# Bringing two column slices of the first input tile by a transposing DMA instead of by TensorE transposes

## The chip, the cores and the metric

The kernel runs on one core of one Trainium2 chip. The metric is the device time of one execution in microseconds (us). A profile is one execution recorded by the hardware profiler; its span is some 2 us shorter than the timed figure.

Names used below: PE is TensorE (matmul), PEld its weight load, DVE is VectorE, ACT is ScalarE, SPq is the queue of SyncE, which issues all DMAs of this kernel. An ft is one of the twelve tiles of 128 columns of w1; four of them make a block. The trace records sixteen landings for each DMA, and these are called its parts.

## The reference, cut to what matters

```python
# x [1, 2048, 640], w1 [640, 1536], w2 [1536, 640], all bf16
h   = silu(einsum("bsd,df->bsf", x, w1))
out = einsum("bsf,fd->bsd", h, w2)
# outputs: out and the gradients of x, w1 and w2 for a given grad_out
```

The kernel works through the 2,048 rows in four chunks of 512. The change concerns only how the first chunk of x gets ready.

## The kernel before

The matmul contracts over the 640 columns of x, which must therefore lie on the partitions: x has to be transposed. Later chunks come by a transposing DMA. For the first chunk, x is loaded as it lies (`x_two`, in two halves of 256 rows), and TensorE transposes it in 128 x 128 pieces. Meanwhile TensorE is kept busy with 22 warm-up matmuls that nobody reads.

```python
KM = 2
NWARM = 22
...
for i in range(NWARM):
    early.append(nc.tensor.matmul(wp[:, 0:P], lhsT=warm[:], rhs=warm[:], start=True, stop=True))
...
early += [load_x_half(0), load_x_half(1), load_w1_rows(0, 1), load_w1_rows(1, KM)]
load_w1_rows(KM, DT)                       # first w1 block: columns 0..511, 5 row slices
start_before_entry_wait(nc, {i.ins.name for i in early})
for fc in range(1, NFC):
    load_w1(fc * FC, (fc + 1) * FC)        # second and third w1 block, 655 KB each
...
nc.sync.dma_start(out=w2_nat[:], in_=w2_v[:])
goT_next = load_goT(0)                     # a transposing DMA
...
def pe_x_half(xT, half):
    lo = half * 2 * P
    for dt_ in range(DT):                  # DT = 5 column slices
        tp = ps_h.tile([P, 2, P], dt_in, name="tp", tag="hp")
        for q in range(2):
            nc.tensor.transpose(tp[:, q, :], x_two[:, half, q, dt_ * P:(dt_ + 1) * P], ident[:])
        copy = nc.scalar.copy if dt_ % 2 else nc.vector.tensor_copy
        copy(out=xT[:, dt_, lo:lo + 2 * P].rearrange("p (s q) -> p q s", q=2), in_=tp[:])

pe_x_half(xT_next, 0)
pe_x_half(xT_next, 1)
...
def h_first(xT, aT, ghT):
    # ft = 0..3 (first w1 block): slices 0..KM-1 for all four, then KM..4 for each;
    # ft = 4..7 need the second w1 block, ft = 8..11 the third
```

So the first 20 hidden-layer matmuls (four ft, five slices) live on the first w1 block. The 21st, the first of ft=4, needs the second block.

## Time and profile before

| | before |
|---|---|
| time, median (first three runs) | 321.44 us |
| span of the profile | 319.4 us |
| PE busy | 314.6 us, 98% |
| both halves of x landed | 3.14 and 4.02 us |
| first hidden-layer matmul | 5.30 us |
| second w1 block: eight of its sixteen parts landed, last part landed | 7.33 us, 9.91 us |
| weight load of the 21st hidden-layer matmul (ft=4) | 9.95 us |

The first excerpt is from the page of before: the span, the busy time of the engines, the chain that ended last by engine and by line, and the group of hidden-layer matmuls (count, busy us, mean ns of one, idle time before them).

```profile
span 319.4 us, 3541 instructions
...
PE 314.6 (98%) x1469; PEld 146.3 (46%) x1498; DVE 102.6 (32%) x182; ACT 77.9 (24%) x142; POOL 0.7 (0%) x6
...
PE 98%; DMA 1%; issue 1%; DVE 0%; DVEq 0%; SPq 0%
PE hp L269 32%; PE hp L206 16%; PE hp L357 16%; PE hp L253 16%; PE hp L406 15%; PE hp L387 1%; DMA x_two<-in_x_dram 1%; PE tp L197 1%; DVE g L398 0%; DVEq L398 0%; SPq L434 0%
...
L206 PE MATMUL hp<-xT,w_nat 128*128 128x512 bf16 x238 | 57.2, 381 | 0.1
```

The chain is PE nearly everywhere. The 1,440 matmuls' worth of work runs 216 ns apart once settled, which is 311 us, so only about 8 us of the span can be won at all, and most of that is the start. The mean of 381 ns is the length of one pipelined matmul, not its spacing.

The chain in order of time, its first pieces (start us, us, what):

```profile
0.09 3.06 DMA x_two<-in_x_dram
3.19 2.31 PE tp L197 x20
5.50 1.93 PE hp L206 x7
7.49 10.74 PE hp L206 x49
```

It starts with the load of x, goes to the 20 transposes, then to matmuls. Now the timeline of the first 12 us (start us, duration us, engine, line, operation, in brackets the idle time before and what ended it):

```profile
0.09 0.87 SPq L173 DMA_DIRECT2D x_two<-in_x_dram  x2
...
1.00 1.44 SPq L178 DMA_DIRECT2D w_nat<-in_w_dram  x3
...
2.48 1.06 SPq L169 DMA_DIRECT2D w_nat<-in_w_dram  x2
...
3.19 2.31 PE L197 MATMUL tp<-ident,x_two 128*128 128x128 bf16 x20 [0.16 <-DMA x_two<-in_x_dram]
...
5.03 12.15 SPq L162 DMA_TRANSPOSE goT<-in_grad_out_dram  x1
...
5.30 6.88 PE L206 MATMUL hp<-xT,w_nat 128*128 128x512 bf16 x28
...
9.95 1.95 PEld L206 LDWEIGHTS <-w_nat 128*128 128x128 bf16 x10 [0.21 <-DMA w_nat<-in_w_dram]
```

Two things are to be seen. TensorE goes from transposes to matmuls without a hole. And the last line shows that the weight load at 9.95 us, the one for ft=4, waited 0.21 us for a DMA of w1: work and data are about level there. PE itself lost nothing by it: its matmuls stay 216 ns apart across that point.

Third, the stretches of one microsecond (us, then busy time of PE, PEld, DVE, ACT and POOL with counts, granted clock, share of the DMA engines, GB/s moved). The view books a packet's whole time and bytes where the packet starts, so a share can pass 1:

```profile
4.00:5.00 1.00, 1.00 (x13) 1.00 (x11) 1.00 (x4) 0.81 (x3) 0.00 (x0) 1.00 0.98 324
5.00:6.00 1.00, 1.00 (x7) 0.60 (x6) 0.99 (x3) 0.77 (x2) 0.00 (x0) 1.00 0.99 347
6.00:7.00 1.00, 1.00 (x5) 0.44 (x4) 0.00 (x0) 0.00 (x0) 0.00 (x0) 1.00 0.97 324
```

The DMA engines are full: 324 to 347 GB/s at a share of 0.97 to 0.99.

### The profile page before, as it was taken

Reading aid. Unit: us, or ns where it says so; the run is one execution under the profiler, and the core shown is the slowest. Engines: PE = TensorE matmul, PEld = TensorE weight load, DVE = VectorE, ACT = ScalarE, POOL = GpSimd, SP = SyncE. Lnnn points to the kernel's source line nnn. Section 1 sums busy time; section 2 is a strip of 40 time slices with the busy share of each in tenths; the row PEclk is TensorE's granted clock in tenths of the full one; section 3 lists DMA queues with packets and bytes.
Section 4 is the critical chain, followed back from the end, with each engine's and each line's share of the span. In section 5 each row is a group of like instructions: output and inputs, shape, how many; then the busy total and the mean of one; then the engine's idle time right before and its main releaser. Section 6 shows DMA issues by size and latency. Waiting matters only on the chain.

```text
span 319.4 us, 3541 instructions
## 1 busy us (share of the span) xinstructions
PE 314.6 (98%) x1469; PEld 146.3 (46%) x1498; DVE 102.6 (32%) x182; ACT 77.9 (24%) x142; POOL 0.7 (0%) x6
## 2 busy tenths in 40 slices
PE   9999999999999999999999999999999999999996
PEld 6444444444444444444444444444444444444443
DVE  3771541477410087710147741000000100001001
ACT  4960000545201254411054520110100001001100
POOL 0000000000000000000000000000000000000000
PEclk9999999999999999999999999999999999999999
DMA  8999999999999855292634079819999998995111
GB/s 282 307 180 222 246 292 264 341 263 292 293 278 271 223 190 140 86 308 76 171 114 133 2 259 267 217 30 294 265 212 257 267 240 292 253 294 182 49 37 45
DMA packets 147312, 67.33 MB, mean 211 GB/s; under 512 B 112609, under 2 KB 147041, under 8 KB 147297
## 3 DMA queue, kind: packets, MB, share of 16 engines
q1 hardware_dynamic: 147296, 67.12, 80.9%
q8 instruction: 11, 0.18, 0.2%
q14 instruction: 5, 0.03, 0.0%
HBM read 9.83 MB, written 28.97 MB: 121 GB/s over the span
## 4 chain that ended last, share of the span: by engine, by line
PE 98%; DMA 1%; issue 1%; DVE 0%; DVEq 0%; SPq 0%
PE hp L269 32%; PE hp L206 16%; PE hp L357 16%; PE hp L253 16%; PE hp L406 15%; PE hp L387 1%; DMA x_two<-in_x_dram 1%; PE tp L197 1%; DVE g L398 0%; DVEq L398 0%; SPq L434 0%
## 5 line engine op out<-in xcount | busy, mean ns | idle before, releaser
L206 PE MATMUL hp<-xT,w_nat 128*128 128x512 bf16 x238 | 57.2, 381 | 0.1
L253 PE MATMUL hp<-goT,w2T 128*128 128x512 bf16 x232 | 56.4, 379 | 0.4
L269 PE MATMUL hp<-aT,w_nat 128*128 128x512 bf16 x235 | 52.2, 379 | 0.3
L269 PE MATMUL hp<-ghT,w1T 128*128 128x512 bf16 x235 | 52.2, 379 | 0.3
L357 PE MATMUL hp<-a_blk,go_nat 128*128 128x512 bf16 x236 | 51.8, 379 | 0.2
L406 PE MATMUL hp<-gh_blk,x_nat 128*128 128x512 bf16 x219 | 48.2, 379 | 0.3
L277 ACT ACTIVATE oT<-hp 128x512 bf16<-128x512 f32 x24 | 14.3, 598 | 109.8 <-PE hp L269 109.8
L215 ACT ACTIVATE aT<-hp 128x512 bf16<-128x512 f32 x48 | 29.9, 625 | 33.0 <-PE hp L206 33.0
L206 PEld LDWEIGHTS <-w_nat 128*128 128x128 bf16 x240 | 23.6, 99 | 28.4 <-issue 0.6
L269 PEld LDWEIGHTS <-w1T 128*128 128x128 bf16 x240 | 23.5, 98 | 28.3
L357 PEld LDWEIGHTS <-go_nat 128*128 128x128 bf16 x240 | 23.5, 98 | 28.3
L253 PEld LDWEIGHTS <-w2T 128*128 128x128 bf16 x240 | 23.5, 98 | 28.3
L269 PEld LDWEIGHTS <-w_nat 128*128 128x128 bf16 x240 | 23.5, 98 | 28.4
L279 DVE CAST oT<-hp 128x512 bf16<-128x512 f32 x16 | 11.1, 692 | 77.0 <-PE hp L269 63.5
L260 DVE SCALAR_TENSOR_TENSOR ghT<-ghT,hp 128x512 bf16<-128x512 bf16 x48 | 32.5, 682 | 7.3 <-PE hp L253 7.3
L406 PEld LDWEIGHTS <-x_nat 128*128 128x128 bf16 x224 | 21.9, 98 | 26.4
L222 DVE SCALAR_TENSOR_TENSOR ghT<-aT,v 128x512 bf16<-128x512 bf16 x48 | 32.8, 687 | 0.5
L221 DVE TENSOR_SCALAR v<-t 128x512 bf16<-128x512 f32 x48 | 20.3, 426 | 30.5 <-ACT t L219 30.5
L219 ACT ACTIVATE t<-hp 128x512 f32<-128x512 f32 x48 | 29.8, 625 | 0.0
L417 DVE CAST g<-hp 128x512 bf16<-128x512 f32 x7 | 4.8, 692 | 47.0 <-PE hp L406 27.4
L367 DVE CAST g2T<-hp 128x512 bf16<-128x512 f32 x7 | 4.8, 692 | 46.1 <-PE hp L357 46.1
L365 ACT ACTIVATE g2T<-hp 128x512 bf16<-128x512 f32 x8 | 4.8, 597 | 47.0 <-PE hp L357 40.8
(20 smaller groups left out, 27.0 us busy)
## 6 DMA issues: line engine op xcount, KB each, us to landing
aT_scr<-aT SPq DMA_DIRECT2D x4, 1536.0 KB, 6.2
ghT_scr<-ghT SPq DMA_DIRECT2D x4, 1536.0 KB, 8.0
out_dram<-o_sb SPq DMA_DIRECT2D x8, 640.0 KB, 3.6
oT_scr<-oT SPq DMA_DIRECT2D x4, 640.0 KB, 3.6
go_nat<-in_grad_out_dram SPq DMA_DIRECT2D x4, 640.0 KB, 6.4
x_nat<-in_x_dram SPq DMA_DIRECT2D x4, 640.0 KB, 5.3
gxT_scr<-oT SPq DMA_DIRECT2D x4, 640.0 KB, 4.7
w_nat<-in_w_dram SPq DMA_DIRECT2D x1, 1920.0 KB, 13.4
```

What stands on the lines that cost most here:

```text
L206: nc.tensor.matmul(hp[:], lhsT=w1_nat[:, dt_, ft * P:(ft + 1) * P], rhs=xT[:, dt_, :], start=(dt_ == 0), stop=(dt_ == DT - 1),)
L215: nc.scalar.activation(aT[:, ft, :], hp[:], ACT.Silu)
L219: nc.scalar.activation(t[:], hp[:], ACT.Tanh, scale=0.5)
L221: nc.vector.tensor_scalar(out=v[:], in0=t[:], scalar1=-0.5, scalar2=0.5, op0=ALU.mult, op1=ALU.add)
L222: nc.vector.scalar_tensor_tensor(out=ghT[:, ft, :], in0=aT[:, ft, :], scalar=1.0, in1=v[:], op0=ALU.subtract, op1=ALU.mult)
L253: nc.tensor.matmul(gp[:], lhsT=w2T[:, dt_, ft * P:(ft + 1) * P], rhs=goT[:, dt_, :], start=(dt_ == 0), stop=(dt_ == DT - 1),)
L260: nc.vector.scalar_tensor_tensor(out=ghT[:, ft, :], in0=ghT[:, ft, :], scalar=1.0, in1=gp[:], op0=ALU.add, op1=ALU.mult)
L269: nc.tensor.matmul(op_[:], lhsT=w_all[:, ft, dt_ * P:(dt_ + 1) * P], rhs=rhs_all[:, ft, :], start=(ft == 0), stop=(ft == FT - 1),)
L277: nc.scalar.activation(oT[:, dt_, :], op_[:], ACT.Copy)
L279: nc.vector.tensor_copy(out=oT[:, dt_, :], in_=op_[:])
L357: nc.tensor.matmul(gp[:], lhsT=go_nat[:, st, dt_ * P:(dt_ + 1) * P], rhs=a_blk[:, st, :], start=(st == 0), stop=(st == ST - 1),)
L406: nc.tensor.matmul(gp[:], lhsT=x_nat[:, st, dt_ * P:(dt_ + 1) * P], rhs=gh_blk[:, st, :], start=(st == 0), stop=(st == ST - 1),)
```

## The change

The intent: take 8 of the 20 transposes and 4 of the 10 copies away from the start. Column slices 3 and 4 of x come by one transposing DMA, placed in the queue behind the first three w1 slices. `KM` becomes 3, so that slices 3 and 4 are needed later. The remaining copies write without a stride.

```diff
-    KM = 2
-    NWARM = 22
+    KM = 3
+    NWARM = 24
+    KT = 3
...
-        early += [load_x_half(0), load_x_half(1), load_w1_rows(0, 1), load_w1_rows(1, KM)]
-        load_w1_rows(KM, DT)
+        early += [load_x_half(0), load_x_half(1), load_w1_rows(0, 1), load_w1_rows(1, KT)]
+        nc.sync.dma_start_transpose(out=xT_next[:, KT:DT, :], in_=x2[0:SC, KT * P:D])
+        load_w1_rows(KT, DT)
...
-            for dt_ in range(DT):
+            for dt_ in range(KT):
...
-                copy(out=xT[:, dt_, lo:lo + 2 * P].rearrange("p (s q) -> p q s", q=2), in_=tp[:])
+                copy(out=xT[:, dt_, lo:lo + 2 * P], in_=tp[:].rearrange("p q s -> p s q"))
```

`x_two` still loads all five column slices, so 512 x 256 elements of x (262 KB) now cross the DMA engines twice.

## The prediction

> **What bounds the kernel now.** TensorE. The page gives PE busy 314.6 of 319.4 us (98%), and the chain of waits is PE for 98%. The chain shows 49 matmuls in 10.74 us, about 216 ns each; 1,440 of them are 311 us. Only some 8 us of the span are other than full-rate matmuls, 5.3 us of them the start, all that the change touches.
>
> **The start of before (timeline and landings).** x half 0 has landed at 3.14 us, half 1 at 4.02. The 20 transposes run from 3.19, 107 ns apart, and the first hidden-layer matmul begins at 5.30. The first three are 420-430 ns apart, from 6.41 on they are 216 ns apart: the array is cold until then. The Trainium skill ("TensorE: Matmul & The Clock Gate", Part 1) puts a cold array at half rate, with a free-running window before it speeds up; the trace agrees (107 ns for 128 columns, 427 for 512). The 21st matmul (ft=4) starts at 10.08. It needs the second w1 block, whose last sixteenth lands at 9.91 (its weight load waited 0.21 us for that DMA); the other fifteen landed by 8.23. So there matmul work and DMA are level already. DMA is saturated: 0.88 to 1.07 busy, 320 to 376 GB/s from 1.5 to 14 us.
>
> **Removes.** 8 transposes (8 x 107 = 0.86 us) and 4 PSUM copies (0.45 us each, DVE and ACT in parallel). Not all is gained: half 1 lands only at 4.02. I expect the first matmul near 5.0, 0.3 us earlier. With dt 0..2 first, the 12 matmuls last to about 8.2, part of them cold.
>
> **Adds.** x still loads whole, so 262 KB more go through a full queue, ahead of the rest of w1. In this trace transposing DMAs run at 290 GB/s at best, so at least 0.9 us. A w2T transpose (655 KB) took 3.1-3.7 us of SyncE issue; scaled, some 1.4 us, so the two last w1 slices are issued near 3.4 instead of 2.0. I estimate xT landing at 6-7.3 us and those slices at 6.5-8.5: level with the need near 8.2. The second w1 block moves from 9.91 to 10.5-11.8. The two more warm-up matmuls are filler.
>
> **On the critical path.** The earlier matmuls then run into the later second w1 block: ft=4 starts near 11.0 instead of 10.08, and everything behind shifts by that. The third block (11.8 us before, needed near 14.4) and w2 (17.0, needed at 18.7) keep their slack. Sum: about +0.9 us.
>
> **Predicted: 322.3 us, range 321.0 to 323.6.** Faster by over 2%: 0.01; within 2%: 0.97; slower by over 2%: 0.02.
>
> **What would show each step.**
> - First hidden-layer matmul at 4.8-5.1 us.
> - xT's transposing DMA landing at 6-7.3 us; second w1 block about 0.6-1.9 us later than 9.91.
> - In the waits, PE or its weight load waits 0.5-1.8 us for w1 before ft=4.
> - From 20 us on, matmul spacing and busy times unchanged; the shift constant to the end.
>
> **What would make it wrong.** (1) The one late DMA engine: if the lag is not there in unprofiled runs, the second block is early enough, and the change gains 0.2-0.4 us. (2) The transposing DMA may hold up the other engines' packets: when goT's begins, packets nearly stop from 15.4 to 16.5 us (24 GB/s in one slice of the DMA view) and w2's sixteen parts land together at 17.0. The same in mid-stream would cost 1-2 us more, and a wait before dt 3. (3) A PE gap could bring the half-rate clock back, 0.2 us per matmul. (4) The cold period may end at another moment (free-running window): 0.2-1 us either way.

## The result, and the profile after

| | before | after |
|---|---|---|
| time, median of 4 runs each (lowest to highest) | 321.28 (321.12 to 321.49) us | 322.34 (321.84 to 322.93) us |
| ratio after : before | | 1.0033, 95% interval 1.0014 to 1.0052 |

A difference given in us below as "above before" is ratio minus one times the median of before of the same rounds. The change costs about 1.1 us, 0.3%. That is "same" at the 2% line, but clear of noise: the interval does not reach 1.

The page after, the same lines (the changed file has two lines more, so L206 of before is L208 here):

```profile
span 321.1 us, 3533 instructions
...
PE 316.1 (98%) x1463; PEld 146.0 (45%) x1492; DVE 101.4 (32%) x180; ACT 76.9 (24%) x140; POOL 0.7 (0%) x6
...
PE 97%; DMA 1%; issue 1%; DVE 0%; SPq 0%; DVEq 0%
PE hp L271 32%; PE hp L208 17%; PE hp L255 16%; PE hp L359 16%; PE hp L408 15%; DMA x_two<-in_x_dram 1%; PE hp L389 1%; DVE xT L201 0%; PE tp L199 0%; SPq L174 0%; DVE g L400 0%; DVEq L400 0%; SPq L436 0%
...
L208 PE MATMUL hp<-xT,w_nat 128*128 128x512 bf16 x233 | 58.7, 390 | 0.5
```

The hidden-layer matmuls have a mean of 390 instead of 381 ns: some of them ran slower. (Their counts differ because a few records are missing in each trace.) The timeline of the start:

```profile
2.05 1.50 SPq L182 DMA_TRANSPOSE xT<-in_x_dram  x1
...
3.25 0.82 PE L199 MATMUL tp<-ident,x_two 128*128 128x128 bf16 x6
3.59 0.57 SPq L179 DMA_DIRECT2D w_nat<-in_w_dram  x1
...
4.21 1.03 SPq L170 DMA_DIRECT2D w_nat<-in_w_dram  x2
...
4.37 0.82 PE L199 MATMUL tp<-ident,x_two 128*128 128x128 bf16 x6 [0.30 <-DMA x_two<-in_x_dram]
...
5.28 6.90 PE L208 MATMUL hp<-xT,w_nat 128*128 128x512 bf16 x20
...
9.07 0.15 PEld L208 LDWEIGHTS <-w_nat 128*128 128x128 bf16 x1 [0.28 <-issue]
9.50 0.15 PEld L208 LDWEIGHTS <-w_nat 128*128 128x128 bf16 x1 [0.28 <-issue]
9.86 2.04 PEld L208 LDWEIGHTS <-w_nat 128*128 128x128 bf16 x10 [0.21 <-issue]
```

The transposes come in two groups with a hole between, because half 1 of x landed at 4.32 us in this run. The first hidden-layer matmul comes at 5.28, as late as before. Then the weight loads stand 0.43 us apart (9.07, 9.50, and so every one since 5.66): the array runs at half rate until about 9.8 us. In before it did so until about 6.3. The weight load for ft=4 comes at 11.59, though the second w1 block had fully landed at 10.97. So in this one profile the block was late, as predicted, and yet PE was later still. Before believing either, one needs more profiles; they follow.

The stretches of one microsecond, columns as before:

```profile
4.00:5.00 1.00, 0.70 (x7) 0.63 (x7) 0.72 (x3) 0.26 (x1) 0.00 (x0) 1.00 1.23 289
5.00:6.00 1.00, 0.91 (x4) 0.29 (x3) 0.65 (x2) 0.37 (x1) 0.00 (x0) 1.00 1.07 219
6.00:7.00 1.00, 1.00 (x4) 0.36 (x3) 0.00 (x0) 0.00 (x0) 0.00 (x0) 1.00 0.99 267
```

The DMA engines moved 219 GB/s from 5 to 6 us where before moved 347.

From the first weight load of the next stage (18.50 us in before, 20.23 after) to the end of the span it is 300.9 us in both profiles, and 300.7 to 300.9 in all fourteen profiles. So all of the loss arises in the first 20 us.

### The profile page after: what moved, and what is told of

It reads as the page before. It is cut to its first block, busy times and chain, and to the rows that moved or that the text cites. A ratio compares the mean times of both kernels' runs of the same rounds, so it can differ in the third digit from the quotient of the medians.

```text
span 321.1 us, 3533 instructions
## 1 busy us (share of the span) xinstructions
PE 316.1 (98%) x1463; PEld 146.0 (45%) x1492; DVE 101.4 (32%) x180; ACT 76.9 (24%) x140; POOL 0.7 (0%) x6
## 4 chain that ended last, share of the span: by engine, by line
PE 97%; DMA 1%; issue 1%; DVE 0%; SPq 0%; DVEq 0%
PE hp L271 32%; PE hp L208 17%; PE hp L255 16%; PE hp L359 16%; PE hp L408 15%; DMA x_two<-in_x_dram 1%; PE hp L389 1%; DVE xT L201 0%; PE tp L199 0%; SPq L174 0%; DVE g L400 0%; DVEq L400 0%; SPq L436 0%
## 5 line engine op out<-in xcount | busy, mean ns | idle before, releaser
L208 PE MATMUL hp<-xT,w_nat 128*128 128x512 bf16 x233 | 58.7, 390 | 0.5
L208 PEld LDWEIGHTS <-w_nat 128*128 128x128 bf16 x240 | 24.1, 100 | 30.0 <-issue 3.2
```

The costliest lines, as they stand in the source:

```text
L208: nc.tensor.matmul(hp[:], lhsT=w1_nat[:, dt_, ft * P:(ft + 1) * P], rhs=xT[:, dt_, :], start=(dt_ == 0), stop=(dt_ == DT - 1),)
```

## The experiments

"Half rate ends" is where the spacing of PE's matmuls halves (from 427 to 216 ns in after; where it falls among the transposes, from 107 to 56 ns, as in e6). The block is the second w1 block, and "half landed" is its eighth part. The last two columns are the weight load for ft=4 and the first weight load of the next stage.

| kernel | time : before, 95% interval | half rate ends | block: half landed | block: last part | ft=4 | next stage |
|---|---|---|---|---|---|---|
| before | | 6.3 | 7.33 | 9.91 | 9.95 | 18.50 |
| after | 1.0033 (1.0014, 1.0052) | 9.8 | 9.05 | 10.97 | 11.59 | 20.23 |
| e1_fill | 1.0049 (1.0033, 1.0066) | 6.0 | 8.96 | 10.34 | 10.38 | 18.82 |
| e2_notrans | 0.9990 (0.9978, 1.0002) | 4.3 | 7.8 | 9.03 | 9.36 | 17.99 |
| e3_notrans_fill | 1.0002 (0.9989, 1.0016) | 5.9 | 7.6 | 8.37 | 9.67 | 18.31 |
| e4_dummyT | 1.0040 (1.0027, 1.0053) | 4.8 | 9.52 | 10.82 | 10.87 | 19.30 |
| e5_slim | 1.0039 (1.0023, 1.0056) | 5.3 | 9.54 | 11.07 | 11.12 | 19.55 |
| e6_dummyP | 0.9997 (0.9980, 1.0015) | 3.7 | 8.94 | 9.65 | 9.70 | 18.13 |
| e7_after2 | 1.0037 (1.0020, 1.0053) | 5.1 | 9.1 | 11.64 | 11.68 | 20.11 |
| e8_after3 | one look, 322.43 us | 4.9 | 9.32 | 11.24 | 11.28 | 19.72 |
| e9_tinyT | 1.0014 (1.0002, 1.0027) | 3.8 | 8.3 | 10.22 | 10.27 | 18.70 |
| e10_issue | 1.0014 (0.9998, 1.0030) | 4.8 | 8.2 | 9.54 | 9.58 | 18.39 |
| e11_lateT | 1.0009 (0.9989, 1.0029) | 9.2 | 8.47 | 8.52 | 11.72 | 20.35 |
| e12_split | 1.0002 (0.9990, 1.0014) | 3.9 | 6.4 and 7.7 | 7.03 and 8.87 | 9.35 | 17.98 |

The medians of before in the three batches (e1 to e4, e5 to e8, e9 to e12) were 320.81, 320.95 and 320.95 us.

There were two theories. COLD: the holes that the change leaves in TensorE's start keep its clock at half rate for longer. DMA: the later second w1 block is what costs, and the clock is chance.

### e1_fill: fill the holes

```diff
-    NWARM = 24
+    NWARM = 25
...
+        def fill(n):
+            wf = ps_h.tile([P, SC], FP32, name="wf", tag="hp")
+            for i in range(n):
+                nc.tensor.matmul(wf[:, 0:P], lhsT=warm[:], rhs=warm[:], start=True, stop=True)
         pe_x_half(xT_next, 0)
+        fill(5)
         pe_x_half(xT_next, 1)
+        fill(3)
```

> The changed kernel with filler matmuls in TensorE's three idle gaps of the start (25 warm-up matmuls, 5 fillers between the transposes of the two x halves, 3 before the first hidden-layer matmul). Theory COLD (the idle gaps keep the array at half rate[...] so 8 more matmuls of 427 instead of 216 ns): the array is fast from about 6.4 us, not 9.9; then the second w1 block (landed at 10.97 after the change) is what ft=4 waits for, so ft=4 starts at 11.0 to 11.2 instead of 11.81 and the kernel still stays 0.6 to 1.1 us above before. Theory DMA (only the later w1 matters, the cold clock is chance): time as the changed kernel, 322.3, and the cold stretch may last to 9.9 all the same.

The result is correct and 1.6 us above before, no better than the change itself. In its profile half rate ended at 6.0 us, and ft=4 waited for the block (last part 10.34, weight load 10.38), as COLD had described for that case, though earlier than its 11.0. But this profiled run was the fastest of its six (321.49 us; the others took 322.05 to 323.01). The loss is above COLD's 0.6 to 1.1 us, but the two theories' times lay too close together for this run to part them. It does show that the loss stays when the holes are filled; so the holes are not the main cause.

### e2_notrans: take the transposing DMA away, leave the holes

```diff
-        nc.sync.dma_start_transpose(out=xT_next[:, KT:DT, :], in_=x2[0:SC, KT * P:D])
+        nc.gpsimd.memset(xT_next[:, KT:DT, :], 0.01)
```

> The changed kernel without its transposing DMA; columns 3 and 4 of xT are set to a constant by GpSimd, so the result is wrong on purpose. DMA bytes are then as in before, TensorE's start with its gaps is as in the changed kernel. COLD: half rate until about 9.9 us again, ft=4 at 11.4 to 11.8, time 0.8 to 1.7 us above before. DMA: the second w1 block lands near 9.9, ft=4 at 10.1 or earlier, time as before (321.3) or up to 0.3 us less.

The result is wrong (relative error 0.33). The time is 0.3 us below before, with an interval that touches no change. COLD said 0.8 to 1.7 us above: it falls. DMA's account holds, and the block came even earlier than it said (9.03 against 9.9, ft=4 at 9.36). The run also bounds the intended gain: even with slices 3 and 4 for nothing, the 8 transposes less (0.86 us of PE in before) bring 0.3 us, and by the interval 0.7 us at most.

### e3_notrans_fill: both away

Both edits above together.

> Both taken away: no transposing DMA (wrong result on purpose) and the gaps filled. Both theories: as before or up to 0.3 us less, first fast matmul near 6.4 us, ft=4 at 9.9 to 10.1. If it is still slower than before by over 0.5 us, a third cause is at work.

As before (1.0002). Expected by both theories; nothing here asks for a third cause.

### e4_dummyT: the transposing DMA alone, in the kernel before

```diff
-    KM = 2
+    KM = 3
...
+        spare = cpool.tile([P, 2, SC], dt_in, name="spare")
+        nc.sync.dma_start_transpose(out=spare[:], in_=x2[0:SC, 3 * P:D])
         load_w1_rows(KM, DT)
```

> The kernel before, with its 20 TensorE transposes, plus the same transposing DMA at the same place of the queue into a spare tile, and the w1 rows split as in the changed kernel (KM = 3). TensorE has no new gaps. DMA: the second w1 block lands near 11.0, PE waits about 0.9 us for it before ft=4, time 0.7 to 1.2 us above before. COLD: the clock goes fast at 6.4 as in before; alone it expects no loss from the clock, time as before, 321.3. If both parts are real, this is the DMA part by itself.

1.3 us above before, with all 20 transposes in place and nothing gained. Half rate ended early, at 4.8 us, and it helped nothing: PE's timeline shows the wait before ft=4.

```profile
5.43 4.48 PE L208 MATMUL hp<-xT,w_nat 128*128 128x512 bf16 x20
10.87 1.47 PE L208 MATMUL hp<-xT,w_nat 128*128 128x512 bf16 x6 [0.96 <-DMA w_nat<-in_w_dram]
```

One transposing DMA, whose data nobody reads, reproduces the whole loss. Now the question is what about it costs: its bytes, or its being a transposing DMA.

### e5_slim: no bytes twice

```diff
-        x_two = cpool.tile([P, 2, 2, D], dt_in, name="x_two")
+        x_two = cpool.tile([P, 2, 2, KT * P], dt_in, name="x_two")
...
-    in_=x2[lo:lo + 2 * P, :].rearrange("(p q) d -> p q d", q=2)
+    in_=x2[lo:lo + 2 * P, 0:KT * P].rearrange("(p q) d -> p q d", q=2)
```

> The changed kernel, but x_two loads only the three column slices that TensorE still transposes, so the 262 KB of columns 3 and 4 are no longer loaded twice; total bytes are as in before. Theory BYTES (the second w1 block is late because 262 KB more go ahead of it): last part of that block lands near 10.2 instead of 10.97 (262 KB at 350 GB/s is 0.75 us), time 0.0 to 0.5 us above before. Theory TRANSPOSE (a transposing DMA in mid-queue costs by itself: all engines are brought into step before it and its packets run slower): the majority of the block's parts still land over 1 us later than before's 7.6, time still 0.6 to 1.2 us above before.

Correct, and 1.3 us above before. Half of the block had landed at 9.54 us, not earlier than in after (9.05), and its last part at 11.07, where BYTES expected 10.2. That is against BYTES and fits TRANSPOSE, but less cleanly than it looks: the narrower loads took SyncE 0.6 to 0.7 us each to issue instead of 0.4, so the block was issued at 4.66 us, not 4.21 as in after. The saved bytes and the later issue may have offset each other. The case against BYTES rests on e6.

### e6_dummyP: the same bytes, plain

```diff
 # against e4
-        nc.sync.dma_start_transpose(out=spare[:], in_=x2[0:SC, 3 * P:D])
+        nc.sync.dma_start(out=spare[:], in_=w1_v[:, 0:2, 0:FC])
```

> The kernel before with the dummy of e4 as a plain load of the same 262 KB (rows of 1,024 B) in the same place. BYTES: as e4, 0.7 to 1.3 us above before, second w1 block about 0.75 us later than before. TRANSPOSE: clearly less than e4, 0 to 0.5 us above before, landings spread as in before and not in step.

As before (0.9997). This is the sharpest pair: e4 and e6 differ in the form of one DMA of 262 KB, and their intervals (1.0027 to 1.0053, 0.9980 to 1.0015) do not meet. With the form comes SyncE's time to issue it (1.61 us in e4, 0.38 in e6), so the block is issued at 4.32 and 2.98 us; e10 below looks at that part. PE's timeline of e6 has one stretch from 5.12 us on. The weight load for ft=4 did wait 0.45 us for the block, but most of that was hidden: between the two matmuls there, PE lost 0.12 us (337 ns instead of 216).

```profile
3.19 1.52 PE L199 MATMUL tp<-ident,x_two 128*128 128x128 bf16 x20 [0.16 <-DMA x_two<-in_x_dram]
5.12 7.13 PE L208 MATMUL hp<-xT,w_nat 128*128 128x512 bf16 x30 [0.41 <-DVE xT L201]
```

The DMA view of 4 to 8 us shows the difference (each figure is a tenth of a microsecond: busy tenths of the DMA engines, then GB/s; both are booked where a packet starts, so a low digit means that few packets started, not that the engines were idle). First e4:

```profile
DMA  9999999999951300099999999995999999999999
GB/s 338 343 346 271 302 284 261 243 161 118 84 59 38 38 20 13 18 169 284 294 294 321 387 315 323 266 154 154 317 358 307 349 348 287 328 297 338 389 307 307
```

Then e6:

```profile
DMA  7678997998999999989696986745897989999999
GB/s 246 246 236 277 307 297 266 348 379 317 400 369 307 369 379 328 379 287 256 246 256 205 276 184 195 205 174 195 246 205 277 358 297 348 379 328 410 358 338 420
```

In e4 the traffic falls to 13 to 38 GB/s from 5.2 to 5.7 us. In e6 it never falls below 174. The packet records tell what happens in that trough. The transposing DMA's packets have 256 bytes and usually take 18 ns. In e4, 19 of those that started between 4.6 and 5.7 us took far longer, up to 1.08 us, and all 19 end between 5.70 and 5.74 us. In after, 14 such packets end within 5.33 and 5.36; in e8, 17 within 5.53 and 5.56. So packets of the transposing DMA that started at different times are let go together at one moment; those that came early waited. What sets that moment, the records do not say. Nor does a trough need a transposing DMA: in e10, whose dummies are plain and tiny (below), traffic falls to 33 GB/s at 5.1 us. The troughs differ in kind. If one counts the packets under way, each from its start to its end, e4 has 17 to 21 in every 0.2 us from 4 to 7 us and after has 15 to 20.5 (before 14.5 to 17), so the engines held packets all the while; in e10 the count falls to 9.5 between 4.6 and 4.8 us, and in e9 to 10.5 between 4.8 and 5.0, so there part of the engines had nothing to do. The load issued ahead of it lands in step too: its sixteen parts came within 0.15 us (5.81 to 5.96) in e4, and spread over 1.45 us (4.62 to 6.07) in e6.

The block's landing answers a question that e6 raises. The plain 262 KB did delay the block: half of it landed at 8.94 instead of 7.33. But its last part landed at 9.65, no later than in before (9.91), because in before one part trailed the others by 1.7 us. PE waits for the last part. Against e2 and e3, where nothing extra goes ahead of the block and no part trails so far, the last part is 0.6 and 1.3 us later (9.03 and 8.37 there). So the bytes do take time, but PE gets to ft=4 at about 9.6 us in e6, and they only use up the slack before that. With the transposing DMA of e4 the block comes at 10.82, past it.

### e7_after2 and e8_after3: the changed kernel again

Unedited; e7 timed in five rounds, e8 one look.

> The changed kernel unedited, to see whether the long cold stretch (half rate to 9.9 us, no wait for w1 before ft=4) of its first profile comes back. If the clock is chance: half rate ends anywhere from 4.4 to 9.9 us, and where it ends early the profile shows a wait for the second w1 block before ft=4. If the cold stretch belongs to the kernel: ends near 9.9 again. Time 322.3 plus or minus 0.4 either way.

> The same once more, one look: a third sample of when the half-rate stretch ends in the changed kernel (chance: another time than 9.9 us).

e7 gives 1.0037, the first result again. In both, half rate ended near 5 us: the long half-rate stretch of the first profile was chance. And in both, ft=4 started 0.04 us after the block's last part. PE's timeline of e8:

```profile
3.19 1.61 PE L199 MATMUL tp<-ident,x_two 128*128 128x128 bf16 x12
4.88 4.61 PE L208 MATMUL hp<-xT,w_nat 128*128 128x512 bf16 x19
11.29 1.04 PE L208 MATMUL hp<-xT,w_nat 128*128 128x512 bf16 x4 [1.80 <-DMA w_nat<-in_w_dram]
```

Here the 1.80 us wait for w1 that the prediction had looked for is in plain sight. The chain that ended last, its long early pieces in e8 (start us, us, what):

```profile
2.05 1.49 SPq L182
4.21 7.03 DMA w_nat<-in_w_dram
11.29 8.81 PE hp L208 x40
```

It no longer starts with x, as in before, but with the 1.49 us in which SyncE issues the transposing DMA; from there it runs through the load of w1 to the matmuls of ft=4. In e7 one part of w1's slices 3 and 4 was late as well (9.35 us), and PE waited for it too.

### e9_tinyT, e10_issue, e11_lateT: which part of the transposing DMA

e9 shrinks the dummy to 128 x 128 elements. e10 puts three tiny plain loads in its place, to have SyncE's issue time without bytes. e11 puts the full dummy behind the second block.

```diff
 # e9, against e4
-        nc.sync.dma_start_transpose(out=spare[:], in_=x2[0:SC, 3 * P:D])
+        nc.sync.dma_start_transpose(out=spare[:, 0, 0:P], in_=x2[0:P, 3 * P:4 * P])
 # e10, against e4
-        nc.sync.dma_start_transpose(out=spare[:], in_=x2[0:SC, 3 * P:D])
+        for j in range(3):
+            nc.sync.dma_start(out=spare[:, j % 2, 32 * j:32 * j + 32], in_=x2[0:P, 32 * j:32 * j + 32])
 # e11, against e4: the dummy moves
-        nc.sync.dma_start_transpose(out=spare[:], in_=x2[0:SC, 3 * P:D])
         load_w1_rows(KM, DT)
+        load_w1(FC, 2 * FC)
+        nc.sync.dma_start_transpose(out=spare[:], in_=x2[0:SC, 3 * P:D])
-        for fc in range(1, NFC): ...
+        for fc in range(2, NFC): ...
```

> e4 with a dummy transpose of 128 x 128 elements (33 KB) instead of 512 x 256 (262 KB), same place. Theory RENDEZVOUS (the transposing DMA's packets on all engines wait until the slowest engine has got there, so fast engines stand idle): most of e4's loss stays although 7/8 of the bytes are gone: first transposing packets end together near 5.5 us, w1's second rows land in step, time 0.4 to 1.0 us above before. Theory SLOW PACKETS (the loss is the 256 B packets' time): about 1/8 of e4's loss, 0 to 0.2 us above before.

> The kernel before with KM = 3 and, in place of the dummy transpose, three tiny plain loads (8 KB each), which cost SyncE about the same issue time (3 x 0.4 us against 1.6 us) and next to no bytes. Theory ISSUE (the loss of e4 is that SyncE issues the next w1 loads over 1 us later): second w1 block later by 0.5 us or more, time 0.4 to 1.2 us above before. RENDEZVOUS: as before, within 0.2 us.

> The full dummy transpose of e4, but issued behind the second w1 block instead of ahead of it (KM = 3). If what counts is that the second w1 block is held up, it lands at 9.0 to 10.0 us again, the third block (needed near 14.4 us) lands late at 12.5 to 14 without a wait, and the time is as before, within 0.2 us. If a transposing DMA in the start costs wherever it stands, 0.7 us or more above before.

e9 lost about 0.45 us (interval 0.06 to 0.87), a third of e4's loss. That lies at the lower edge of RENDEZVOUS's range and above that of SLOW PACKETS; the load ahead of it did land in step (5.10 to 5.25 us), but none of its 128 packets waited, against RENDEZVOUS. e10 also shows about 0.45 us, with an interval that includes no loss; its issue took 1.33 us on SyncE, against 1.17 in e9 and 1.61 in e4. In both e9 and e10 the block was issued at 3.9 us, against 2.5 in before, and in both part of the engines ran dry (above). In e10's profile it was not late (9.54 us), against what ISSUE expected; but that run took 321.03 us, the second fastest of six that reach to 322.40. So e9's loss, and some of e4's, may be nothing but issue time; these runs do not settle it. By the middle values the larger part of e4's loss needs the full-sized transposing DMA, and e4's engines did not run dry; but the intervals of e4 and e9 touch (at 1.0027). The wait of its packets for a common moment and their small size come together there, and I have no run that parts them.

e11 is clearer: the median is that of before (320.99 against 320.95). The same DMA that costs 1.3 us ahead of the second block costs nothing that can be told behind it. Its packets waited there just as long (16 of them, up to 1.13 us, all ending between 8.33 and 8.37 us in its profile), but the block had been issued before them and landed at 8.52. One of its six runs took 323.02 us, and that was the profiled one: a part of x came at 5.01 us, the transposes paused for 0.9 us, and half rate lasted to 9.2. That one run widens e11's interval to 1.0029, so that it overlaps e4's by a hair. So a late x together with a long half rate can go with a loss of 2 us, but it is not what separates the two kernels.

### e12_split: a try for something faster than both

```diff
-        for fc in range(1, NFC):
-            load_w1(fc * FC, (fc + 1) * FC)
+        for lo, hi in ((0, 2), (2, DT)):
+            nc.sync.dma_start(out=w1_nat[:, lo:hi, FC:2 * FC], in_=w1_v[:, lo:hi, FC:2 * FC])
+        for fc in range(2, NFC):
+            load_w1(fc * FC, (fc + 1) * FC)
```

> A try for a version faster than both: before, with the second w1 block loaded in two pieces (row slices 0 and 1, then 2 to 4), so that ft=4 can start on the first piece. Before waited for that block at about 10 us with little slack, so 0 to 0.3 us less than before is expected; no theory above expects a loss.

As before (1.0002). No kernel beats before beyond noise; e2, which is wrong, shows how little there was to win by this road.

## Why the prediction was right or wrong, point by point

- **Total: right.** 322.3 was predicted, 322.34 measured, inside 321.0 to 323.6, and within 2%.
- **The place: right.** The loss sits at ft=4, on the second w1 block, in two of three profiles of the changed kernel. It is a constant shift afterwards (300.9 us from the next stage to the end, in before and after).
- **The block's landing: right.** Predicted 10.5 to 11.8; measured 10.97, 11.64 and 11.24. xT landed at 6.59 to 6.81 in the three profiles (predicted 6 to 7.3).
- **ft=4: under-sized.** Predicted near 11.0; its first matmul came at 11.81, 11.68 and 11.29.
- **The first matmul: about right.** 5.28, 4.92 and 4.88 against 4.8 to 5.1. As foreseen, half 1 of x sets it (landed 4.32, 3.97 and 3.93).
- **The reason given for the later block: wrong.** The step reads: "262 KB more go through a full queue, ahead of the rest of w1", worth at least 0.9 us. The same bytes as a plain load cost no time clear of noise (e6: 0.9997, by the interval 0.5 us at most); they bring the block to 9.65 us, level with PE, and not past it. What costs is the DMA being a transposing one in front of that block (e4: block at 10.82, 1.3 us lost; against e6 and e11). The prediction had a mechanism of this kind, packets held up, but as a risk under its second "what would make it wrong", which was to cost 1 to 2 us on top of the bytes; it should have been the term itself. The sum came out right by luck, because the wrong term had about the right size.
- **SyncE's issue time: right in size, its worth open.** 1.4 us was estimated, 1.49 measured (after), and the last two w1 slices were issued at 3.59 us (predicted near 3.4). How much of the loss it makes is not shown: e10, which has such an issue time and no transposing DMA, lost 0.45 us, with an interval from none to 1.0 us.
- **The clock: a named risk, its point (4), that came true in one profile.** It made the first profile of the changed kernel look like a clock problem. Only the repeats and e2 showed that this was chance.
- **The late part: seen again.** One or two of the block's sixteen parts trailed in most profiles (in after the eighth landed at 9.05, the last at 10.97), so PE sees the slowest part, not the bandwidth. Unprofiled runs show no landings, but the loss is there in them too (after 321.84 to 322.41, before 321.12 to 321.49).

## What to carry to other kernels

In this kernel a DMA's cost in a full queue was not its bytes alone: what counted was what stood behind it, when that was needed, and whether the DMA was a transposing one. Put a transposing DMA behind the loads that the next wait is for. And before a start of a few microseconds is explained from one profile, profile the same kernel again: here the first one told of a cause that the second and third did not have.

## What the Trainium skill lacked or had wrong

- "DMA: Bandwidth & Descriptors", Rules for kernel authors, says that a transpose next to ordinary DMAs needs nothing. That concerns correctness, and the results here were correct; on what it does to the time of the DMAs around it the page has no word. Here the first packets of a transposing DMA waited up to 1.08 us and ended together within 0.04 us, the load ahead of it landed in step, and the traffic fell to 13 GB/s for a moment (e4). The kernel lost 0.40%, against nothing that can be told for the same bytes as a plain load.
- The same page, Latency and other measured facts, gives 261 GB/s for a transposing DMA of one kind. The runs agree: in after xT's last part landed 1.02 us behind that of the load ahead of it, so 262 KB in 1.02 us, an estimate of 257 GB/s.
- The same section ascribes slower engines, as a best guess, to one kind of DMA, which the SyncE queue is not. In this kernel, all on SyncE's queue, one part of the block came 1.7 us (before) and 1.7 us (e8) after the fifteenth. The trace does not name the engine.
- "TensorE: Matmul & The Clock Gate", Part 1, says that the window is free-running and that the moment the clock rises varies by run, by 500 ns either way around some 4 us of matmul activity. The traces agree that it varies, but by far more: the first matmul runs at 0.5 us, and half rate ended between 3.7 and 9.8 us in fourteen profiles of nearly the same start; in e6 and before, where PE had paused no more than 0.2 us until then, at 3.7 and 6.3. The granted clock of the profile's views stood at 1.00 in those stretches all the same (before, 4 to 6 us); the half rate is to be read from the spacing of the matmuls.
- No page has the issue time of a transposing DMA on SyncE by its size for this chip (the DMA page has one cycle count, for small tiles). Here it took 1.17 us for 128 x 128 elements, 1.3 to 1.6 for 512 x 256 (2.8 in e11, one place further back in the queue), while the plain load of the same 262 KB took 0.38.
